# Batch 0's u built transposed in PSUM, with its token form by two DMA transposes, and channel weights loaded in three-chunk pieces

## The chip, the cores and the metric

The kernel runs on one core of a Trainium2 chip. A core has five engines with instruction streams of their own: TensorE (PE, matmuls; its weight loads are PEld), VectorE (DVE), ScalarE (ACT), GpSimd (POOL) and SyncE (SP, which here only issues transfers). Matmul results go to PSUM, eight banks of 128 x 512 floats. The metric is device time in microseconds (us).

## The reference, cut to what matters

```python
# linear attention with decay; q, k, v, alpha: (4, 8, 768, 48)
for t in range(S):
    state = alpha[:, :, t, :, None] * state + einsum('bhd,bhe->bhde', k[:, :, t], v[:, :, t])
    y[:, :, t] = einsum('bhd,bhde->bhe', q[:, :, t], state)
x = y.transpose(0, 2, 1, 3).reshape(B, S, H * D)          # (4, 768, 384)
# mixer
h  = np.maximum(x.transpose(0, 2, 1) @ w_tok1, 0.0) @ w_tok2   # over tokens, 768 -> 256 -> 768
u  = x + h.transpose(0, 2, 1)
h2 = np.maximum(u @ w_ch1, 0.0) @ w_ch2                        # over channels, 384 -> 1536 -> 384
out = u + h2
```

## The kernel before, in words

There are four batches b. Each has three attention chunks of 256 tokens, n = 3b to 3b + 2, whose outputs are six x tiles of 128 tokens by 384 channels (x0_n and x1_n), and then one mixer pass.

`attention(n)` loads alpha, k, q and v (ld_at, ld_kt, ld_qt, ld_vt). The first three chunks take the "wide" form: the log of alpha (ln, ScalarE), a cumulative sum by matmul (cumw), its exponentials E and IE, the scaled keys and queries kk and qq, their TensorE transposes trk and trq with the copies evk and evq, the products G0 and G1 with their masks, the state K with sa and sm, and y0, y1 with the parts from the former state (ia, ib). vb, vs, ka, kb and kc are casts and half turns of v and k. Chunks 6 to 11 transpose by DMA instead (dk, dq).

`mixer(b)` has these operations:

- t1_b_m_kc: six matmuls for each of two halves m of the 256 token features; ht_b_m is the ReLU.
- t2_b_i: for each token tile i, two matmuls into one bank, tokens on the partitions; u_b_i, on VectorE, adds x and writes u.
- The channel product needs u with channels on the partitions (ut). Batch 0 (the tuple UP) does this with TensorE transposes, up_0_p, 18 in all, and three copies ut_0_p. Batches 1 to 3 use two DMA transposes ux_b_half on SP's queue.
- c1_b_mc_half: three matmuls for each of twelve chunks mc of 128 channel features and each half of the tokens; rt_b_mc_half is its ReLU, on ScalarE or VectorE.
- c2_b_i_q4: twelve matmuls for token tile i in four groups; o_b_i adds u (VectorE), st_b_i stores. The last batch's tile 0 is done in two column halves (0h0, 0h1).

Weights come by ldw_ (384 KB each) and are cast by cw_: wt1 in two pieces, wt2 in two (by its 256 input rows), wc1 in six (128 input rows by 768 columns; pieces 0 to 2 are the left half of the columns, 3 to 5 the right), wc2 in six. A c1 of mc below 6 needs wc1 pieces 0, 1 and 2, the others 3, 4 and 5. Loads and weights share 19 raw buffers ("in"); a load waits until its buffer's former use is over.

Nothing is scheduled on the chip. ORDER is a list written out by a planner: each word is an operation and the engine that runs it (t PE, s ACT, v DVE, g POOL, y SP), so each engine's own sequence is that of its words in the list. BUFS gives the buffer numbers. The words f1_, f2_, f3_, f4_, f8_ are filler matmuls on zeros (`fill`, N units of 512 columns), placed ahead of the operation named. Operations marked port=True on VectorE and GpSimd are put one behind the other where the engine changes (`shared`).

Of the kernel before, what the change touches and what calls it, by code (L numbers as in the profile page):

```python
# [9 lines left out]
BF16 = mybir.dt.bfloat16  # L10
# [84 lines left out]
B, H, S, D = 4, 8, 768, 48  # L95
# [6 lines left out]
UP = (0,)  # L102
# [18 lines left out]
def build(g):  # L121
# [194 lines left out]
    def mixer(b):  # L316
# [27 lines left out]
        uts = []
        if b in UP:
            for p in range(3):
                bank = V("one")
# [4 lines left out]
                uts.append(P.op(f"ut_{b}_{p}", either(dve(768, True), act(768)), m0 + (3950 + 340 * p) * sc, writes=[ut],
                                reads=[bank], preds=[o], emit=lambda e, p=p, bank=bank: g.utev(e, ut, bank, p)))
        else:
            for half in range(2):
# [4 lines left out]
        rts = []  # L360
        for mc in range(NDC):
            rt = V("rt")
            ro = []
            for half in range(2):
                bank = V("one")
                o = P.op(f"c1_{b}_{mc}_{half}", pe([384] * 3), m0 + (4900 + 975 * mc + 487 * half) * sc, writes=[bank],
                         reads=[ut], preds=(uts[0:2 + half] if b in UP else [uts[half]]) + [wl[("wc1", p)] for p in ((0, 1, 2) if mc < 6 else (3, 4, 5))],
# [5 lines left out]
        for i in range(NS):  # L373
            hold = 4000.0 if (i >= NS - 3 and b < B - 1) else 0.0
            cuts = [(0, HD // 2), (HD // 2, HD)] if (b, i) == LAST else [(0, HD)]
            for ci, (ca, cz) in enumerate(cuts):
# [3 lines left out]
                for q4 in range(4):  # L380
                    pp = []
                    for mc in range(3 * q4, 3 * q4 + 3):
# [6 lines left out]
                          reads=[bank, us[i][0]], preds=[prev],  # L389
# [25 lines left out]
trq2t ld_at3y vs1_2g ldw_wt11y evq2v ib1t y1_1t y0_1t vs0_2g ldw_wt21y sm1_1g P3g K2t sa0_2v sm0_2g x0_1s t1_0_0_0t
f1_G0_2t G0_2t ldw_wt20y G1_2t cw_wt20g t1_0_1_0t mask0_2v x1_1s t1_0_1_1t ld_at4y ld_kt3y t1_0_1_2t lnP3s cum3t
cw_wt11s IE3s ia2t y0_2t x0_2s t1_0_0_1t t1_0_0_2t E3s t1_0_0_3t mask1_2v t1_0_1_3t ib2t y1_2t ldw_wc14y t1_0_1_4t
x1_2s t1_0_0_4t f1_t1_0_1_5t t1_0_1_5t ht_0_1v P4g cw_wt21s t1_0_0_5t ht_0_0s f3_t2_0_0t t2_0_0t t2_0_1t u_0_0v ln13s
r13s ldw_wc13y t2_0_2t u_0_1v t2_0_3t u_0_2v t2_0_5t lnP4s t2_0_4t u_0_3v u_0_5v u_0_4v up_0_0t cw_wc14s cw_wc13s
ldw_wc15y up_0_1t ld_qt3y k0a3g kk3g cum4t trk3t cw_wc15g ut_0_0v up_0_2t ut_0_2v ut_0_1s c1_0_11_0t c1_0_8_0t IE4s  # L420
c1_0_11_1t rt_0_8_0v rt_0_11_0v ldw_wc11y q0r3g qq3g c1_0_9_1t rt_0_9_1v ln14s kb3s c1_0_10_0t cw_wc11s c1_0_9_0t
# [544 lines left out]
```

## Time and profile before

The median of three runs is 163.35 us (163.22 to 163.51). The profiled execution has a span of 160.5 us from its first to its last instruction, 2.85 us below that median; what lies outside the span is in the time of a run.

| engine | busy us | share of the span | instructions |
|---|---|---|---|
| TensorE matmuls | 154.6 | 96% | 1563 |
| VectorE | 114.9 | 72% | 206 |
| ScalarE | 97.8 | 61% | 179 |
| GpSimd | 80.8 | 50% | 94 |

In the profile, L with a number is a line of the kernel: a group is named by line, engine, operation and out<-in. Through helpers many operations share a line; L643 is every small matmul and the fillers, L902 is c1, L907 c2, L878 t1, L883 t2, L894 up, L712 trk and trq. In the view of stages, each engine has its busy us and in brackets its instructions; then come the granted TensorE clock, the DMA share and GB/s. In the timeline, a row is start, length and instruction, in brackets the idle time ahead of it and what ended that. The chain of work is followed back from the last instruction.

### The profile page before, as it was taken

The numbers are of one execution on the slowest core, as the hardware profiler recorded it, in microseconds if no ns is written. First come the engines' busy times: TensorE is split into PE (matmuls) and PEld (weight loads), VectorE is DVE, ScalarE is ACT, GpSimd is POOL, SyncE is SP. The second block draws the span as 40 slices with busy tenths as digits, with TensorE's granted clock in tenths as the row PEclk, the third lists the DMA queues.
The fourth block names the chain that finished last, engine by engine and source line by source line (L and its number), as shares of the span: only waits on it lengthen the run. The fifth ranks groups of instructions, "written<-read, shape, count | busy, mean of one in ns | idle before, by whom it ended". The sixth has DMA issues, their size and how long they took to land.

```text
span 160.5 us, 3971 instructions
## 1 busy us (share of the span) xinstructions
PE 154.6 (96%) x1563; PEld 97.1 (60%) x1563; DVE 114.9 (72%) x206; ACT 97.8 (61%) x179; POOL 80.8 (50%) x94
## 2 busy tenths in 40 slices
PE   7999989999999999999999999999999999999992
PEld 2545565766667676666667666566567665665661
DVE  6099994979889787989969758795886762464222
ACT  3789999998899955897563583269832203343000
POOL 5205897695973649389778852699523000000000
PEclk9999999999999999999999999999999999999999
DMA  4999999999999999999989999989701235111133
GB/s 122 320 324 317 317 374 311 339 333 306 316 347 324 275 278 272 210 228 319 241 202 298 239 315 204 217 196 134 196 21 62 87 79 169 49 49 53 49 129 116
DMA packets 76130, 35.05 MB, mean 218 GB/s; under 512 B 70352, under 2 KB 74320, under 8 KB 76112
## 3 DMA queue, kind: packets, MB, share of 16 engines
q1 hardware_dynamic: 73808, 31.76, 74.1%
q10 hardware_dynamic: 2304, 3.05, 5.3%
q8 instruction: 12, 0.20, 0.5%
q14 instruction: 6, 0.05, 0.1%
HBM read 25.17 MB, written 4.72 MB: 186 GB/s over the span
## 4 chain that ended last, share of the span: by engine, by line
PE 61%; DMA 12%; DVE 6%; ACT 6%; SPq 6%; POOL 4%; issue 3%; DVEq 0%; POOLq 0%
PE ps L907 22%; PE ps L902 21%; PE ps L643 11%; DMA in<-in_v_dram 6%; SPq L584 6%; DMA out_dram<-o 4%; PE ps L878 3%; PE ps L883 2%; DMA ut<-u 2%; DVE pkk L700 2%; DVE gtm L770 1%; PE ps L712 1%; DVE rt L875 1%; POOL vb L746 1%; POOL pkq L700 1%
## 5 line engine op out<-in xcount | busy, mean ns | idle before, releaser
L907 PE MATMUL ps<-wc,rt 128*128 128x384 bf16 (+1 forms) x300 | 52.4, 319 | 0.0
L902 PE MATMUL ps<-ut,wc 128*128 128x384 bf16 x288 | 50.3, 326 | 0.1
L902 PEld LDWEIGHTS <-wc 128*128 128x128 bf16 x288 | 27.1, 98 | 17.9 <-DMA ut<-u 0.6
L907 PEld LDWEIGHTS <-rt 128*128 128x128 bf16 x300 | 27.8, 98 | 16.0
L873 ACT ACTIVATE rt<-ps 128x384 bf16<-128x384 f32 x47 | 21.4, 492 | 23.6 <-PE ps L902 23.3
L875 DVE TENSOR_SCALAR rt<-ps 128x384 bf16<-128x384 f32 x49 | 25.6, 551 | 9.1 <-PE ps L902 8.9
L770 DVE TENSOR_TENSOR gtm<-ps,mk 128x1024 bf16<-128x1024 f32 x24 | 28.5, 1218 | 3.1 <-PE ps L643 2.8
L911 DVE TENSOR_TENSOR o<-ps,u 128x384 f32<-128x384 f32 (+1 forms) x25 | 13.2, 536 | 12.6 <-PE ps L907 10.1
L700 POOL TENSOR_TENSOR pkk<-in,IE 128x768 bf16<-128x768 f32 x8 | 14.5, 1817 | 3.3 <-DVE ss L844 2.3
L745 ACT CAST x<-ps 128x384 bf16<-128x384 f32 x20 | 9.2, 479 | 11.1 <-PE ps L643 9.5
L887 DVE TENSOR_TENSOR u<-ps,x 128x384 bf16<-128x384 f32 x24 | 12.0, 550 | 3.1 <-PE ps L883 2.5
L746 POOL CAST vb<-in 64x384 bf16<-64x384 f32 (+1 forms) x14 | 8.3, 594 | 10.4 <-DMA in<-in_v_dram 4.7
L692 POOL TENSOR_TENSOR in<-in,in 128x384 f32<-128x384 f32 x8 | 8.0, 1000 | 10.5 <-DVE u L887 3.8
L643 PE MATMUL ps<-rt 128*128 128x512 bf16 (+1 forms) x29 | 12.1, 515 | 1.1 <-DVE rt L541 1.1
L745 ACT CAST vb<-in 64x384 bf16<-64x384 f32 (+1 forms) x18 | 11.4, 634 | 0.8 <-DMA in<-in_v_dram 0.3
L700 POOL TENSOR_TENSOR pkq<-in,E 128x768 bf16<-128x768 f32 x6 | 10.9, 1818 | 0.6 <-DMA tpk<-pkq 0.3
L878 PE MATMUL ps<-x,wt 128*128 128x384 bf16 x48 | 11.0, 325 | 0.0
L844 POOL TENSOR_TENSOR ss<-tmp,E 128x384 bf16<-128x384 f32 x10 | 8.3, 833 | 4.2 <-DVE in L628 3.9
L841 DVE TENSOR_TENSOR tmp<-ps,ss 128x384 f32<-128x384 f32 x16 | 8.8, 552 | 1.8 <-PE ps L643 0.6
L883 PE MATMUL ps<-ht,wt 128*128 128x384 bf16 x48 | 9.1, 326 | 0.0
L643 PE MATMUL ps<-vb,gtm 128*128 128x48 bf16 x192 | 8.2, 183 | 0.2 <-DVE gtm L770 0.2
L643 PE MATMUL ps<-tpq,tpk 48*64 48x128 bf16 (+1 forms) x288 | 7.9, 218 | 0.4 <-POOL tpq L746 0.3
(94 smaller groups left out, 207.6 us busy)
## 6 DMA issues: line engine op xcount, KB each, us to landing
in<-in_alpha_dram SPq DMA_DIRECT2D x12, 384.0 KB, 5.1
in<-in_v_dram SPq DMA_DIRECT2D x12, 384.0 KB, 5.6
in<-in_k_dram SPq DMA_DIRECT2D x12, 384.0 KB, 5.2
in<-in_q_dram SPq DMA_DIRECT2D x12, 384.0 KB, 5.5
in<-in_moe_w_ch_dram SPq DMA_DIRECT2D x12, 384.0 KB, 5.9
out_dram<-o ACTq DMA_DIRECT2D x15, 192.0 KB, 1.8
in<-in_moe_w_tok_dram SPq DMA_DIRECT2D x4, 384.0 KB, 6.0
out_dram<-o SPq DMA_DIRECT2D x8, 192.0 KB, 2.2
```

Of the source, the lines that this page charges most:

```text
L643: return self.pe.matmul(out, lhsT=lhsT, rhs=rhs, start=start, stop=stop, skip_group_check=True)
L700: self.shared(self.eng[e].tensor_tensor(self.t(dst)[:, :, h0:h1, 0:D], self.t(src)[:, h0:h1].rearrange("p h s d -> p s h d"), bass.AP(tens ...
L745: return self.act.copy(d, s)
L770: self.nc.vector.tensor_tensor(self.t(gtm)[:, hf, :, :], self.pair(gp).rearrange("p a (j t) -> p (a j) t", t=128), bass.AP(tensor=m.tensor ...
L873: self.act.activation(d, s, AF.Relu)
L875: self.nc.vector.tensor_scalar_max(d, s, 0.0)
L878: self.pe.matmul(self.bank(bank)[:, 0:HD], lhsT=self.wt1[:, kc, m * 128 : m * 128 + 128], rhs=self.t(x), start=(kc == 0), stop=(kc == NS - 1))
L883: self.pe.matmul(self.bank(bank)[:, 0:HD], lhsT=self.wt2[:, kc, i * 128 : i * 128 + 128], rhs=self.t(hts[kc]), start=(kc == 0), stop=(kc = ...
L887: self.nc.vector.tensor_tensor(self.t(u)[:, i % 3], self.bank(bank)[:, 0:HD], self.t(x), ALU.add)
L902: self.pe.matmul(self.bank(bank)[:, 0:HD], lhsT=self.wc1[:, kc, mc * 128 : mc * 128 + 128], rhs=self.t(ut)[:, 3 * half : 3 * half + 3, kc, ...
L907: self.pe.matmul(self.bank(bank)[:, 0 : cz - ca], lhsT=self.t(rts[mc][0])[:, i * 128 : i * 128 + 128], rhs=self.wc2[:, mc, ca:cz], start=( ...
L911: self.nc.vector.tensor_tensor(self.t(o)[:, ca:cz], self.bank(bank)[:, 0 : cz - ca], self.t(u)[:, i % 3, ca:cz], ALU.add)
```

## The change

For batch 0 alone (UDIR), u is no longer made with tokens on the partitions. For each half of the tokens and each of three channel groups j, one bank takes three matmuls of x against the identity (xa_0_half_j, 128 columns each), which put x in transposed, and then two matmuls of 384 columns of ht against wt2 (tt_0_half_j), which add h transposed. The copy ut_0_half_j (ScalarE or VectorE) writes it as ut. The u that o needs comes from two DMA transposes of ut on SP's queue (un_0_half), put side by side in the queue. t2, u, up and the old ut of batch 0 are gone; the other batches keep theirs.

wc1 is loaded in pieces of 256 columns with all three chunks of 128 input rows, and wt2 in two pieces by output tokens. A c1 needs only the piece of its mc // 2, a t2 or tt only that of its half. The contiguous runs are 1 KB and 1.5 KB instead of 3 KB.

ORDER and BUFS are new from the first word to the last. The fillers are fewer (21 units instead of 36), loads come in another order, many operations change their engine, stores on SP fall from nine to five, and the DMA transposes stand closer together in SP's queue.

```diff
-UP = (0,)
+UP = ()
+UDIR = (0,)
...
+        if b in UDIR:
+            ut, us, uts = V("ut"), [], []
+            for half in range(2):
+                evs = []
+                for j in range(NM):
...
+                    xa = P.op(f"xa_{b}_{half}_{j}", pe([128] * 3), ..., writes=[bank],
+                              reads=[v for v, _ in tx], preds=[o for _, o in tx], ...)
+                    o = P.op(f"tt_{b}_{half}_{j}", pe([384] * 2), ..., writes=[bank],
+                             reads=[h for h, _ in hts], preds=[h for _, h in hts] + [xa, wl[("wt2", half)]], ...)
+                    evs.append(P.op(f"ut_{b}_{half}_{j}", either(act(384), dve(384)), ..., writes=[ut], reads=[bank], preds=[o], ...))
+                uts.append(evs)
                 u = V("u")
+                un = P.op(f"un_{b}_{half}", {"SP": (1240.0, 1240.0)}, ..., writes=[u], reads=[ut], preds=evs, ...)
+                us += [(u, un)] * 3
...
-    ... + [wl[("wc1", p)] for p in ((0, 1, 2) if mc < 6 else (3, 4, 5))],
+    ... + [wl[("wc1", mc // 2)]],
...
-            c, h = piece % 3, piece // 3
-            self.gated(dma(t, self.w[2][128 * c : 128 * c + 128, 768 * h : 768 * h + 768]), op)
+            w = self.w[2].rearrange("(c p) m -> p c m", p=128)
+            self.gated(dma(t.rearrange("p (c m) -> p c m", c=3), w[:, :, 256 * piece : 256 * piece + 256]), op)
...
+    def xadd(self, bank, xs, j):
+        for i, x in enumerate(xs):
+            self.mm(self.bank(bank)[:, i * 128 : i * 128 + 128], self.t(x)[:, j * 128 : j * 128 + 128], self.idn, i == 0, False)
+
+    def tok2t(self, bank, half, j, hts):
+        for kc in range(NDT):
+            self.mm(self.bank(bank)[:, 0:HD], self.t(hts[kc])[:, j * 128 : j * 128 + 128],
+                    self.wt2[:, half, kc, :], False, kc == NDT - 1)
+
+    def utev3(self, e, ut, bank, half, j):
+        self.copy(e, self.t(ut)[:, 3 * half : 3 * half + 3, j, :], self.bank(bank)[:, 0:HD].rearrange("p (i t) -> p i t", i=3))
+
+    def unat(self, u, ut, half):
+        self.nc.sync.dma_start_transpose(self.t(u).rearrange("p i (j c) -> p (i j) c", j=NM),
+                                         self.t(ut)[:, 3 * half : 3 * half + 3].rearrange("p i j t -> p (i j t)"))
```

The order up to the first c1 of batch 0, before:

```
ld_at1y ld_at0y ln1s ln0s f8_cumw1t f1_cumw1t cumw1t IE1s cumw0t IE0s ld_vt0y E0s vb0g vs0_0g vs1_0v ld_kt0y kk0v
f8_trk0t f1_trk0t trk0t E1s ld_qt0y qq0v ka0s kb0s kc0v f1_trq0t trq0t ld_kt1y kk1v K0t evq0s s0_0v ld_vt1y vb1s
f1_trk1t trk1t ld_at2y evk0v ln2s f2_G0_0t G0_0t ld_qt1y ka1g sa1_0v f4_cumw2t cumw2t mask0_0v vs0_1s kb1g kc1g vs1_1s
K1t sm1_0g qq1v sa0_1v sm0_1v G1_0t ld_kt2y IE2s E2s trq1t evq1s ib0t mask1_0v f3_y1_0t y1_0t y0_0t evk1v G0_1t sa1_1v
ld_qt2y x1_0s mask0_1v G1_1t ld_vt2y x0_0s vb2s kk2g trk2t kc2s ldw_wt10y qq2g cw_wt10s f2_ia1t ia1t mask1_1v evk2s
trq2t ld_at3y vs1_2g ldw_wt11y evq2v ib1t y1_1t y0_1t vs0_2g ldw_wt21y sm1_1g P3g K2t sa0_2v sm0_2g x0_1s t1_0_0_0t
f1_G0_2t G0_2t ldw_wt20y G1_2t cw_wt20g t1_0_1_0t mask0_2v x1_1s t1_0_1_1t ld_at4y ld_kt3y t1_0_1_2t lnP3s cum3t
cw_wt11s IE3s ia2t y0_2t x0_2s t1_0_0_1t t1_0_0_2t E3s t1_0_0_3t mask1_2v t1_0_1_3t ib2t y1_2t ldw_wc14y t1_0_1_4t
x1_2s t1_0_0_4t f1_t1_0_1_5t t1_0_1_5t ht_0_1v P4g cw_wt21s t1_0_0_5t ht_0_0s f3_t2_0_0t t2_0_0t t2_0_1t u_0_0v ln13s
r13s ldw_wc13y t2_0_2t u_0_1v t2_0_3t u_0_2v t2_0_5t lnP4s t2_0_4t u_0_3v u_0_5v u_0_4v up_0_0t cw_wc14s cw_wc13s
ldw_wc15y up_0_1t ld_qt3y k0a3g kk3g cum4t trk3t cw_wc15g ut_0_0v up_0_2t ut_0_2v ut_0_1s c1_0_11_0t
```

and after, to where the weights catch up:

```
ld_at0y ln0s f8_cumw0t f1_cumw0t cumw0t ld_at2y ln2s E0s cumw2t ld_qt0y qq0v f2_trq0t trq0t ld_kt0y IE0s kk0v ka0v
kb0v IE2s ld_vt1y vb1g ld_vt0y vb0g vs1_0g vs0_0g vs0_1g evq0s trk0t evk0v G1_0t mask1_0v vs1_1s kc0s G0_0t mask0_0v
ld_at1y ln1s E2s cumw1t IE1s ld_kt2y kk2v K0t s0_0v y0_0t f2_ib0t ib0t y1_0t E1s ld_kt1y kk1v kb1s ld_qt1y qq1v sa1_0v
sm1_0g ka1s f1_trk1t trk1t kc1s trk2t evk2v ld_qt2y qq2g trq1t evq1v x1_0s evk1s K1t sa0_1v sm0_1g f4_G0_1t G0_1t
mask0_1v kc2s ld_vt2y vb2s vs0_2g sa1_1v sm1_1g f2_trq2t trq2t x0_0s ia1t ldw_wt10y ldw_wt20y G1_1t evq2s ld_at3y P3g
y0_1t x0_1s K2t cw_wt10s mask1_1v sa0_2v sm0_2g f1_G0_2t G0_2t ib1t y1_1t x1_1s G1_2t ln13s t1_0_1_0t xa_0_0_0t
t1_0_0_0t t1_0_0_1t t1_0_0_2t t1_0_1_1t t1_0_1_2t ia2t mask0_2v y0_2t lnP3s cum3t ib2t ldw_wt11y cw_wt11s t1_0_0_3t
IE3s mask1_2v vs1_2g y1_2t x1_2s E3s ldw_wt21y xa_0_0_2t x0_2v t1_0_1_3t t1_0_1_4t t1_0_0_4t t1_0_1_5t t1_0_0_5t
ht_0_0s xa_0_1_0t xa_0_1_2t xa_0_0_1t xa_0_1_1t cw_wt21g cw_wt20g ht_0_1v tt_0_1_2t tt_0_0_1t tt_0_0_0t tt_0_0_2t
tt_0_1_1t ld_kt3y ldw_wc10y k0a3v r13s ut_0_0_1s kk3v tt_0_1_0t trk3t ut_0_0_2s cw_wc10g ld_qt3y q0r3g ut_0_0_0v
c1_0_0_0t c1_0_1_0t ldw_wc12y cw_wc12s c1_0_5_0t ut_0_1_2v evk3v ut_0_1_0s ut_0_1_1v c1_0_5_1t rt_0_5_1v ldw_wc15y
```

Later words of the new order: the loads from the 23rd are vt3, at4, wc14, wc13, at5, kt4 and wc11; SP's queue has "ld_at6y un_0_1y un_0_0y ld_at7y" with "o_0_4v", "o_0_3v" and "o_0_2v" among them and mask0_5v behind; ahead of ux_2_0y it has all loads but qt11, and st_0_4 and st_1_1, before two stores just ahead of ux_2, are gone from there.

More of the change, by code (lines that the diff above doesn't have):

```diff
@@ L366, in mixer @@
                 o = P.op(f"c1_{b}_{mc}_{half}", pe([384] * 3), m0 + (4900 + 975 * mc + 487 * half) * sc, writes=[bank],
[L367 removed]
+                         reads=[ut], preds=(uts[half] if b in UDIR else uts[0:2 + half] if b in UP else [uts[half]]) + [wl[("wc1", mc // 2)]],
                          emit=lambda e, mc=mc, half=half, bank=bank: g.ch1(bank, ut, mc, half))
@@ L415 @@
[L415 to L419, printed above, removed]
```

201 lines of the change are left out of this document (106 added, 95 removed), and 22 rows, old and new, of the table BUFS.

## The prediction

> **What bounds the kernel now.** I read the page's busy line first, then busy time by stage, then TensorE's timeline through the first 32 us, and there the other engines and the loads.
>
> ```profile
> span 160.5 us, 3971 instructions
> PE 154.6 (96%) x1563; PEld 97.1 (60%) x1563; DVE 114.9 (72%) x206; ACT 97.8 (61%) x179; POOL 80.8 (50%) x94
> ```
>
> ```profile
> 1.06:31.76 30.70, 29.45 (x318) 16.61 (x319) 23.13 (x51) 26.13 (x40) 18.00 (x25) 1.00 1.06 313
> 31.76:157.44 125.68, 125.19 (x1246) 80.44 (x1246) 91.20 (x153) 71.46 (x140) 62.38 (x64) 1.00 0.75 200
> 157.44:160.50 3.06, 0.00 (x0) 0.00 (x0) 0.36 (x1) 0.00 (x0) 0.00 (x0) 1.00 0.27 96
> ```
>
> From 31.76 us, where the channel product of batch 0 begins, TensorE (first busy column) stands still for 125.68 - 125.19 = 0.49 us until its last matmul. The amount of real matmul work hardly changes, so the time follows from when that packed stretch begins and whether it stays packed. Ahead of it TensorE only looks busy, because of the filler matmuls, which read rt:
>
> ```profile
> 1.06 4.21 PE L643 MATMUL ps<-rt 128*64 128x384 f32 x7 [1.06 <-DVE rt L541]
> ...
> 7.34 2.26 PE L643 MATMUL ps<-rt 128*64 128x384 f32 x7
> 9.73 0.62 PE L712 MATMUL ps<-idn,pkk 128*128 128x128 bf16 x8
> ...
> 25.58 0.37 PE L643 MATMUL ps<-vb,gtm 128*128 128x48 bf16 x8
> ...
> 26.94 0.86 PE L643 MATMUL ps<-rt 128*64 128x384 f32 x2
> 27.73 2.28 PE L883 MATMUL ps<-ht,wt 128*128 128x384 bf16 x12
> 29.85 0.83 PE L894 MATMUL ps<-idn,u 128*128 128x128 bf16 x12
> 30.52 0.33 PE L643 MATMUL ps<-la,u 128*128 128x384 bf16 x1
> ...
> 30.81 0.61 PE L712 MATMUL ps<-idn,pkk 128*128 128x128 bf16 x8
> 31.25 0.50 PE L894 MATMUL ps<-idn,u 128*128 128x128 bf16 x6
> 31.76 0.48 PE L902 MATMUL ps<-ut,wc 128*128 128x384 bf16 x2
> ```
>
> The opening is set by VectorE and by the loads:
>
> ```profile
> 8.33 0.35 DVE L746 CAST vb<-in 64x384 bf16<-64x384 f32 x1 [4.26 <-POOL vb L746]
> 8.72 0.96 DVE L700 TENSOR_TENSOR pkk<-in,IE 128x768 bf16<-128x768 f32 x1
> 12.21 0.68 DVE L746 COPY tpk<-ps 128x1024 bf16<-128x1024 bf16 x1
> 12.80 0.55 DVE L841 TENSOR_TENSOR tmp<-ps,ss 128x384 f32<-128x384 f32 x1
> ...
> 23.17 2.36 DVE L770 TENSOR_TENSOR gtm<-ps,mk 128x1024 bf16<-128x1024 f32 x2
> 26.88 0.56 DVE L875 TENSOR_SCALAR ht<-ps 128x384 bf16<-128x384 f32 x1 [1.36 <-PE ps L878]
> 28.27 2.88 DVE L887 TENSOR_TENSOR u<-ps,x 128x384 bf16<-128x384 f32 x6 [0.83 <-PE ps L883]
> ```
>
> ```profile
> 4.28 0.84 ACT L637 ACTIVATE la<-in 128x768 bf16<-128x768 f32 x1 [2.19 <-DMA in<-in_alpha_dram]
> 6.32 0.81 ACT L687 ACTIVATE IE<-ps 128x768 f32<-128x768 f32 x1
> 11.26 1.31 ACT L745 COPY tpq<-ps 128x1024 bf16<-128x1024 bf16 x1 [0.47 <-PE ps L712]
> 25.99 0.48 ACT L745 CAST x<-ps 128x384 bf16<-128x384 f32 x1
> 30.72 0.80 ACT L745 COPY ut<-ps 128x768 bf16<-128x768 bf16 x1 [0.17 <-PE ps L894]
> ```
>
> ```profile
> 18.61 1.82 POOL L700 TENSOR_TENSOR pkq<-in,E 128x768 bf16<-128x768 f32 x1
> 23.37 0.83 POOL L844 TENSOR_TENSOR ss<-tmp,E 128x384 bf16<-128x384 f32 x1
> 30.16 0.88 POOL L746 CAST wc<-in 128x768 bf16<-128x768 f32 x1 [0.36 <-DMA in<-in_moe_w_ch_dram]
> ```
>
> The first load lands at 4.28. The cast at 30.16 had waited for wc15, the 22nd load in the queue, so a load lands every (30.16 - 4.28) / 21 = 1.23 us, and the nth at about 4.28 + 1.23 (n - 1). VectorE works without a gap from 8.33 (vs1_0) to the end of the third chunk's masks at 25.53. Before, c1_0 with mc of 6 or more needs wc13, wc14 and wc15, thus it could not begin before 30.16 + 0.88 = 31.04, whatever the transposes did.
>
> **The change part by part.** *The opening, walked by hand through the new order, with these durations.* The log of at0 ends at 5.15, cumw0 at 6.3 (5.17 to 6.32 before), E0 (0.83) at 7.15. qt0 is now third (6.74), so qq0 runs 7.2 to 8.15, 1.5 us ahead of the first product before. kk0 9.1, trk0 9.7, evk0 10.4; evq0 on ScalarE (trq0 8.8, then 1.31) 10.1; G1_0 10.9, its mask (2.36 / 2) 12.1, the next 13.3, kk2 14.2. at1 is only seventh (11.66): log 12.5, cumw1 13.65, IE1 14.5. Then VectorE is packed: s0_0 14.7, kk1 15.6, qq1 16.5, sa1_0 17.0, evk2 17.65, evq1 18.9, sa0_1 19.4, mask0_1 20.6, sa1_1 21.1, mask1_1 22.3, sa0_2 22.8, mask0_2 23.9, mask1_2 25.1. On GpSimd sm1_0, qq2 (1.82) and sm0_1 end at 17.8, 19.65 and 20.5, just in time. y1_2 (0.37) 25.45, x1_2 25.95. Before, the last x ended at 26.47: 0.5 us is gained, of a 1.5 us earlier start, because at1 comes late.
>
> *Tail of batch 0's token product.* Before, 27.73 - 26.47 = 1.26 us pass from x1_2 to the first t2; the same gives 27.2 for the first tt. Twelve tt matmuls take what twelve t2 took (29.85 - 27.73 = 2.1): 29.3, trk3 (31.25 - 30.81 = 0.44) 29.7. The eighteen up transposes are gone from here (0.67 + 0.51 = 1.2 us). The eighteen xa matmuls of 128 columns cost 1.0 at the pace of the up transposes (0.67 / 12 each), in the two waits, for the last x and for ht, where the filler of 26.94 stood; without that cover 1.0 comes back. VectorE loses six u additions (2.9) and two ut copies and takes three of the six new ones; ScalarE one ut (0.80) for three like x (0.48 each). None of that ends last.
>
> *Weights in three-chunk pieces.* c1_0_0 and c1_0_1 need only wc10, the 19th load: 26.4, and its GpSimd cast, which stands behind kk3 on VectorE (28.45), ends at 29.3. So c1_0 starts at 29.7 instead of 31.76. cum4, 30.81 - 30.52 = 0.29, is then still to do: the lead is 2.06 - 0.29, some 1.8 us. Runs of 1 KB and 1.5 KB in place of 3 KB I put at nothing:
>
> ```profile
> in<-in_moe_w_ch_dram SPq DMA_DIRECT2D x12, 384.0 KB, 5.9
> in<-in_moe_w_tok_dram SPq DMA_DIRECT2D x4, 384.0 KB, 6.0
> ```
>
> wt1 already comes in 1 KB runs and lands in about the time of the 3 KB ones; the bounds are -0.1 and +0.1 us a load, hidden but for the pieces waited for. The next pieces keep up:
>
> ```profile
> 70.74 2.44 PE ps L902 x15
> ```
>
> A ch1 group of three costs 2.44 / 5 = 0.49. wc15 (22nd, 30.1 plus 0.9 of cast) is wanted after four groups, at 31.65. The tightest is wc11, the 29th: 38.7 plus 0.9, wanted after 18 groups, trq3, the two G of chunk 3 (0.8) and cum4, at 29.7 + 8.8 + 0.4 + 0.8 + 0.3 = 40.0.
>
> *Fillers.* 36 units of 512 columns become 21 (N in fN). Fifteen fewer, at the 2.26 / 9 us of the second row above, are 3.8 us. That is the most the opening can give; the walk turns about half of it into idle time.
>
> *The two un transposes* stand in SP's queue behind ld_at6 and ahead of ld_at7.
>
> ```profile
> 59.29 1.61 SPq L584 DMA_DIRECT2D in<-in_v_dram  x1
> 62.89 1.33 SPq L725 DMA_TRANSPOSE tpk<-pkk  x1
> ...
> 85.63 2.17 SPq L584 DMA_DIRECT2D in<-in_v_dram  x1
> ...
> 93.33 3.16 SPq L624 DMA_DIRECT2D out_dram<-o  x2
> 96.97 3.29 SPq L729 DMA_TRANSPOSE ut<-u  x2
> ```
>
> ```profile
> DMA to landing us min/median/max: 2.8/3.0/3.8
> ```
>
> Two take 3.29 us of issue in the last of the queue's rows, and land 3.0 us after (the answer for ux). They read ut copies made some 20 us earlier, so they wait for nothing; behind them at7, kt6 and at8 shift by 3.3 us, and o_0_4, o_0_3 and o_0_2 wait for them on VectorE, ahead of mask0_5. at6, the 41st load, is issued near 4.28 + 1.23 * 40 - 5.9 = 47.6, the pair by 50.9, landed by 54. c2_0_2_3, the last product ahead of o_0_2, falls near 54 too. I take nothing; without that cover, up to 3 us of VectorE, part of it on the path.
>
> *Everything else in the order* is moved too: 54 of 96 rt evacuations change engine, four stores leave SP for ScalarE, dk and dq stand closer in SP's queue. The data chains stay the same. The idle time after c1's start was 0.49; for the new order I allow 0.3 more, the bounds being 0.5 less and the whole lead.
>
> The end is o and the half store as before (3.06 us), issued by ScalarE: nothing. Sum: 160.5 - 1.8 + 0.3 = 159.0 of span. The runs' median 163.35 is 2.85 above the profiled span, so 161.85.
>
> **The rivals.** *TensorE runs at half rate in the opening (slower).* The same nine filler units took 4.21 us from 1.06 and 2.26 from 7.34, though the granted clock is 1.00 in both rows: after standing idle the array is slower. In my walk it works only some 2 of 5.2 us from 7.4 to 12.6, where the nine-unit filler stood. If it falls back there, cumw1 costs 1.0 more, trk1, trk2 and trq1 0.5 each, and the four units of f4 ahead of G0_1 another 1.0: about 3 us until 19. That is 163.35 - 1.5 + 3 = 164.8. It decides once it lasts past about 17 us. Against it: no single gap in the walk is over 1.5 us. The Trainium skill, "TensorE: Matmul & The Clock Gate", Part 1: The HAM clock gate, has the array fall to half rate after an idle window of about 3.4 us, which would leave it at full rate here and the time at 161.85. Its section "A second HAM failure mode: psum-queue depth-cycling" says that frequent short idles can do it too, which would give this rival's time. This case's trace shows the cold start alone.
>
> *The queue of transfers becomes the bound.* Before ux_2_0 SP has 63 loads (62 before) and two more transposes: 1.23 + 3.29 = 4.5 us more. Two stores ahead of ux_2 (3.16, the row at 93.33) leave the queue. Net 1.4 later, while TensorE wants it 1.5 earlier: 163.35 - 1.5 + 2.9 = 164.75 if SP has no slack; with the slack that it shows (from 60.9, the end of the row at 59.29, it stands 2.0 us ahead of dk6), about 163.3. For it: the loads run at their pace between the rows of 85.63 and 93.33 five loads take 7.7 us of issue. Against: those waits move with the compute.
>
> *The opening starts no earlier*: c1_0 still waits for casts, and only the 0.5 us of x1_2 stays: 162.9.
>
> **How the numbers follow.** Forecast 0.58 (160.4, where most of the 3.8 us shows, to 162.9); half rate 0.17 (164 to 165.5); queue 0.20 (163.0 to 164.75; of it 0.02 faster, 0.06 same, 0.12 slower); no earlier 0.05 (0.03 faster, 0.02 same). With 0.01 of the forecast on the slow side: faster 0.62, same 0.08, slower 0.30. 0.2% is about what a measurement can tell from no change. The range of 8 in 10 is 160.4 to 164.6.
>
> **What would show it.** Right: qq0 near 7.2, the last mask of chunk 2 near 25, the first ch1 matmul near 29.7, its cast just before, less than 1 us of idle from there to the last matmul. Half rate: cumw1's four large products near 13 us taking twice what cumw0's take near 5. Queue: ch1 of batch 2 waiting for ut. The un pair: VectorE's o waiting for a transfer into u near 55 us. The prediction is wrong if the packed stretch starts by 30 but is itself more than 1.5 us longer than 125.7.

## The result, and the profile after

The changed kernel takes 170.57 us (median of 4 runs, 168.88 to 170.97) where the kernel before took 163.28 (162.63 to 163.51) beside it: 1.044 times as long, 95% interval 1.0383 to 1.0498. The prediction was 161.85 with a range of 160.4 to 164.6; the time lies well above it. The profiled execution took 170.76 us, its span is 169.1. Where single executions of a kernel took more than 1.5% longer than its fastest, the times and ratios from here on leave them out.

In the changed kernel lines stand lower down: the matmul helper L643 is now L669, c1 L902 is L944, c2 L907 is L949, o L911 is L953, the copies L745/L746 are L771/L772, the loads L584 are L608, dk and dq L725 are L751, ux L729 is L755, and un is the new L939. First the page's busy line, then busy time by stage (the first pair after the time is the stage's length and TensorE's busy time; the last three numbers are granted clock, DMA share and GB/s).

```profile
span 169.1 us, 3962 instructions
PE 154.6 (91%) x1552; PEld 98.0 (58%) x1552; DVE 111.2 (66%) x197; ACT 97.2 (57%) x180; POOL 83.9 (50%) x99
```

```profile
1.06:30.66 29.60, 26.50 (x301) 16.74 (x302) 22.68 (x49) 23.10 (x36) 14.31 (x24) 0.94 1.07 310
30.66:165.94 135.28, 128.06 (x1255) 81.25 (x1252) 87.99 (x146) 73.80 (x145) 69.14 (x71) 0.99 0.77 192
165.94:169.10 3.16, 0.00 (x0) 0.00 (x0) 0.36 (x1) 0.00 (x0) 0.00 (x0) 1.00 0.42 152
```

TensorE is busy for the same 154.6 us as before. The opening is 1.10 us shorter (30.66 against 31.76), the end 0.10 longer, and the stretch that was packed grew from 125.68 to 135.28: -1.10 + 9.60 + 0.10 = 8.6, which is the difference of the spans. In that stretch TensorE now stands still 135.28 - 128.06 = 7.22 us, against 0.49; the other 2.87 us of the 9.60 are busy time. Its timeline shows where; the bracket names the idle time ahead of a row and what ended it.

```profile
56.25 0.40 PE L669 MATMUL ps<-tpq,tpk 48*128 48x128 bf16 x8 [0.68 <-DVE o L953]
...
69.41 0.34 PE L669 MATMUL ps<-vb,pkk 128*128 128x96 bf16 x4 [1.69 <-ACT pkk L771]
...
73.89 5.52 PE L944 MATMUL ps<-ut,wc 128*128 128x384 bf16 x33 [0.41 <-DMA ut<-u]
...
84.65 0.64 PE L669 MATMUL ps<-tpq,tpk 48*64 48x128 bf16 x32 [0.49 <-POOL tpq L772]
...
92.11 0.90 PE L949 MATMUL ps<-wc,rt 128*128 128x384 bf16 x3 [2.25 <-DVE o L953]
...
122.46 0.64 PE L669 MATMUL ps<-tpq,tpk 48*64 48x128 bf16 x32 [1.09 <-ACT tpq L771]
```

Behind the stand of 2.25 us the granted clock falls to half, and 3.5 us pass at 0.53 of the clock, which is some 1.6 us lost, and more than half of that added busy time:

```profile
90.00:92.50 2.50, 0.39 (x3) 0.19 (x2) 1.00 (x3) 0.41 (x2) 1.26 (x2) 0.97 1.10 271
92.50:96.00 3.50, 3.40 (x51) 2.14 (x50) 2.61 (x4) 2.52 (x4) 1.79 (x3) 0.53 1.03 292
```

Who is late? Five of these six stands lead back to a DMA transpose that landed late. The sixth (92.11) leads to an o tile, whose former content VectorE had to see stored first, with a late transpose right behind it. Here is SP's queue (start, time to issue), and then what VectorE, ScalarE and GpSimd waited for (total, times, longest):

```profile
48.02 6.05 SPq L939 DMA_TRANSPOSE u<-ut  x2
...
60.54 2.08 SPq L608 DMA_DIRECT2D in<-in_v_dram  x1
63.46 2.06 SPq L751 DMA_TRANSPOSE tpk<-pkk  x1
...
74.17 2.68 SPq L608 DMA_DIRECT2D in<-in_alpha_dram  x2
76.94 3.36 SPq L751 DMA_TRANSPOSE tpk<-pkq  x1
...
83.69 2.33 SPq L608 DMA_DIRECT2D in<-in_v_dram  x2
86.37 2.11 SPq L751 DMA_TRANSPOSE tpk<-pkk  x1
```

```profile
DVE o L953 <- DMA out_dram<-o: 4.3, 2, 2.6
...
ACT pkk L771 <- DMA tpk<-pkk: 2.4, 1, 2.4
ACT tpq L771 <- DMA tpk<-pkq: 2.3, 1, 2.3
...
POOL tpq L772 <- DMA tpk<-pkq: 1.6, 1, 1.6
...
DVE o L953 <- DMA u<-ut: 1.0, 1, 1.0
```

The answers for single issues give 7.1 and 4.2 us from issue to landing for the un pair, 5.4 for dk6 (63.46), 6.3 for dq7 (76.94), 6.7 for dk8 (86.37) and 6.2 for the dk at 113.46. The two lines below group all dk and dq, the first of the kernel before, the second of the changed one:

```profile
DMA to landing us min/median/max: 2.7/3.0/5.9
```

```profile
DMA to landing us min/median/max: 2.8/3.6/6.7
```

Before, the latest landing (5.9) was that of the dq at 104.16, right behind the load at 103.65:

```profile
103.65 0.42 SPq L584 DMA_DIRECT2D in<-in_q_dram  x1
104.16 1.87 SPq L725 DMA_TRANSPOSE tpk<-pkq  x1
```

In the changed kernel the six that take longer than 5.2 us are all issued within 0.9 us of the end of a load's issue. The dq at 115.94 (5.1) stands behind the late dk of 113.46; the stand at 122.46 comes by way of it.

### The profile page after: what moved, and what is told of

It is laid out like the page before. It is cut to its first block, busy times and chain, and to the rows that moved or that the text cites. A ratio compares the mean times of both kernels' runs of the same rounds, so it can differ in the third digit from the quotient of the medians.

```text
span 169.1 us, 3962 instructions
## 1 busy us (share of the span) xinstructions
PE 154.6 (91%) x1552; PEld 98.0 (58%) x1552; DVE 111.2 (66%) x197; ACT 97.2 (57%) x180; POOL 83.9 (50%) x99
## 4 chain that ended last, share of the span: by engine, by line
PE 58%; DMA 23%; DVE 3%; ACT 2%; POOL 2%; SPq 2%; issue 1%; DVEq 0%
PE ps L949 19%; PE ps L944 16%; PE ps L669 13%; DMA tpk<-pkk 7%; DMA tpk<-pkq 7%; PE ps L904 5%; DMA u<-ut 4%; PE ps L909 3%; DMA in<-in_q_dram 2%; DMA ut<-u 2%; PE ps L738 2%; SPq L751 2%; ACT tpq L771 2%; POOL pkk L726 1%; DVE o L953 1%
## 5 line engine op out<-in xcount | busy, mean ns | idle before, releaser
L949 PE MATMUL ps<-wc,rt 128*128 128x384 bf16 (+1 forms) x300 | 54.8, 323 | 2.3 <-DVE o L953 2.3
L944 PE MATMUL ps<-ut,wc 128*128 128x384 bf16 x288 | 51.7, 326 | 0.6 <-DMA ut<-u 0.6
L899 ACT ACTIVATE rt<-ps 128x384 bf16<-128x384 f32 x51 | 23.8, 491 | 28.9 <-PE ps L944 27.8
L949 PEld LDWEIGHTS <-rt 128*128 128x128 bf16 x300 | 28.0, 98 | 18.8 <-issue 3.0
L944 PEld LDWEIGHTS <-wc 128*128 128x128 bf16 x288 | 26.9, 98 | 18.3 <-issue 0.9
L901 DVE TENSOR_SCALAR rt<-ps 128x384 bf16<-128x384 f32 x45 | 23.6, 553 | 17.0 <-PE ps L944 16.9
L953 DVE TENSOR_TENSOR o<-ps,u 128x384 f32<-128x384 f32 (+1 forms) x25 | 13.0, 538 | 16.2 <-PE ps L949 10.9
L870 POOL TENSOR_TENSOR ss<-tmp,E 128x384 bf16<-128x384 f32 x13 | 10.9, 836 | 17.9 <-DVE tmp L867 11.3
L726 POOL TENSOR_TENSOR pkq<-in,E 128x768 bf16<-128x768 f32 x8 | 14.5, 1814 | 0.6
L771 ACT CAST vb<-in 64x384 bf16<-64x384 f32 (+1 forms) x20 | 13.0, 656 | 2.7 <-DVE o L953 2.1
L772 POOL CAST vb<-in 64x384 bf16<-64x384 f32 (+1 forms) x16 | 8.9, 563 | 8.1 <-DVE kt L772 7.4
L669 PE MATMUL ps<-tpq,tpk 48*64 48x128 bf16 (+1 forms) x288 | 8.8, 228 | 3.4 <-ACT tpq L771 1.3
L771 ACT CAST x<-ps 128x384 bf16<-128x384 f32 x16 | 7.5, 474 | 6.6 <-PE ps L669 6.5
L726 POOL TENSOR_TENSOR pkk<-in,IE 128x768 bf16<-128x768 f32 x6 | 10.9, 1817 | 0.7 <-ACT IE L705 0.5
L669 PEld LDWEIGHTS <-tpk 48*64 48x64 bf16 (+1 forms) x288 | 6.5, 108 | 7.3 <-issue 4.0
L913 DVE TENSOR_TENSOR u<-ps,x 128x384 bf16<-128x384 f32 x18 | 8.8, 549 | 1.2 <-PE ps L909 1.2
L669 PE MATMUL ps<-rt 128*128 128x512 bf16 (+1 forms) x18 | 8.6, 582 | 1.1 <-DVE rt L565 1.1
L669 PE MATMUL ps<-vb,gtm 128*128 128x48 bf16 x192 | 9.0, 188 | 0.0
L654 POOL TENSOR_TENSOR in<-in 128x384 f32<-128x384 f32 x8 | 7.9, 998 | 1.0 <-DVE in L718 0.8
```

The source lines that it names most:

```text
L669: return self.pe.matmul(out, lhsT=lhsT, rhs=rhs, start=start, stop=stop, skip_group_check=True)
L726: self.shared(self.eng[e].tensor_tensor(self.t(dst)[:, :, h0:h1, 0:D], self.t(src)[:, h0:h1].rearrange("p h s d -> p s h d"), bass.AP(tens ...
L771: return self.act.copy(d, s)
L772: return self.shared(self.eng[e].tensor_copy(d, s))
L870: self.shared(self.eng[e].tensor_tensor(self.st(self.t(s)), self.st(self.t(t)), self.amul(E, hf, wide), ALU.mult))
L899: self.act.activation(d, s, AF.Relu)
```

## The experiments

The theory that this suggests, "behind loads": a DMA transpose that SP issues right after loads lands in 5 to 7 us and not in 3, and the new order puts the un pair, dk6, ux_1, dq7, dk8 and one dk at 113 in that place. The rivals: transposes side by side slow each other; the un pair alone moved everything; o and its stores; the half clock.

**The cost by itself.** A kernel that only issues groups of transposes and loads, fully drained in between.

```diff
+CASES = ("T", "TT", "TTT", "LT", "LLT", "LLLLT", "LLLLTT", "TLLLL", "LLLLTLLLL", "LLTLLT", "WWWWT", "T")
```

> Nothing of the reference is computed here: only DMA transposes (T, 128 x 1024 of bf16, as dk and dq) and loads (L, 384 KB of q, k, v or alpha; W, of the channel weights) are issued from SP's queue, in groups with a full drain between them: T; TT; TTT; LT; LLT; LLLLT; LLLLTT; TLLLL; LLLLTLLLL; LLTLLT; WWWWT; T. Theory 'behind loads': a transpose by itself lands some 2.8 us after its issue (the median of before), in TT and TTT all land in 3 to 3.6, and what stands behind loads lands the later the more of them are outstanding: LLT 4 to 5, LLLLT and LLLLTT 5 to 7; in TLLLL the T keeps its 2.8. Rival 'side by side': T behind loads keeps 2.8 to 3.3 in all groups, and it is the second and third T of TT and TTT that land in 5 to 7 us.

Landing, in us: T 3.1; TT 3.2, 3.1; TTT 3.3, 3.5, 3.2; LT 4.1; LLT 4.9; LLLLT 4.7; LLLLTT 4.8, 3.2; TLLLL 3.2; LLLLTLLLL 4.7; LLTLLT 4.6, 4.7; WWWWT 6.1; T 3.0. (The median of dk and dq before is 3.0, as shown above, not the 2.8 of the expectation.) SP's rows of LT, LLT and LLLLT (line numbers of that kernel) show that the issue grows too, from the 1.24 to 1.34 of a transpose with nothing ahead:

```profile
19.92 1.70 SPq L41 DMA_TRANSPOSE tp<-pk  x1
...
26.16 2.61 SPq L41 DMA_TRANSPOSE tp<-pk  x1
...
35.49 2.40 SPq L41 DMA_TRANSPOSE tp<-pk  x1
```

Side by side costs nothing; behind loads costs 1.0 to 1.8 us, and 3.0 behind weights, less than "behind loads" had said for four loads, since its price does not grow past two of them. What follows the transpose does not matter (TLLLL).

**The same in the kernel before**, one move (the diffs of the order show SP's words alone, without the engine's letter):

```diff
 ld_qt8 ld_at10
+ld_vt8 ld_at11 ld_qt9
 dk8 dq7 dk7 st_0_2 dq8
-ld_vt8 ld_at11 ld_qt9
```

> The kernel before with one thing of the new order: the loads vt8, at11 and qt9 stand ahead of dk8, dq7 and dk7 in SP's queue, not behind them (their buffers are long free). Theory 'behind loads': dk8 lands in 5 to 7 us after its issue instead of 2.7 to 3.0, and TensorE, which stood 0.49 us in the whole packed stretch, stands 1 to 4 us more near 80 to 86: 164 to 167. Rival 'side by side': nothing changes at dk8; 163.0 to 163.7.

169.41 us (167.56 to 169.87) against 162.02 to 164.32 (163.18) of the kernel before beside it, ratio 1.0372 (1.0295 to 1.0449): more than either theory gave. dk8 lands in 5.2 us. SP, GpSimd and TensorE:

```profile
79.64 2.94 SPq L725 DMA_TRANSPOSE tpk<-pkk  x1
```

```profile
87.00 0.50 POOL L746 COPY pkk<-pkk 64x384 bf16<-64x384 bf16 x1 [6.31 <-DMA tpk<-pkk]
```

```profile
87.55 0.34 PE L643 MATMUL ps<-vb,pkk 128*128 128x96 bf16 x4 [3.56 <-POOL pkk L746]
```

dk8, dq7 and dk7 are late one behind the other, and the copy of kc7 waits for the last of them. The medians lie 6.2 us apart, where the whole change costs 7.3. Not all of it is shown to be the move's. The profile is of the fastest execution (167.56). In it TensorE is already 1.25 us behind the kernel before at its first c1 (33.01), which the move does not touch. Matmul for matmul it is 1.46 us behind at 79.4, and 5.2 to 5.6 us from behind the stand at 87.55 on. So some 3.9 us are the move's there. The 1.25 stay unexplained; executions of the kernel before differ by more. Part of the price is the issue of the three loads itself: dk8 is issued 4.05 us later than before (75.59), 1.46 of which was there already.

**The changed kernel without the un pair.**

```diff
-emit=lambda e, u=u, half=half: g.unat(u, ut, half)
+emit=lambda e: None
```

> The changed kernel without the two transposes that make batch 0's token form: o of batch 0 adds u in its transposed form instead, which costs the same and gives other values in batch 0's output. All else is in the changed order. Theory 'behind loads' (the transposes land late because of the loads issued just ahead of them, and un is only two of them): the 6.05 us of SP's queue at 48 us are gone, with them TensorE's 0.68 at 56 us and, since loads at7 to vt7 now come 6 us earlier and have landed by the time dk6 is issued, the 1.69 and 0.41 at 69 to 74; dq7, dk8 and dk10 still stand right behind loads, so the 0.49 at 84.65, the 2.25 with the half clock behind it at 92, and the 1.09 at 122 stay: 170.6 - 2.8 = 167.8, and 167 to 169. Rival 'it is the un pair': everything downstream follows from the shift of the loads by 6 us, and the packed stretch comes back to some 126.5 us: 162 to 163.5.

This kernel leaves out the making of the token form; o adds ut as it lies, so batch 0's output is not that of the reference. 169.16 us, ratio 1.0385 (1.031 to 1.046), 0.2 us above the theory's range. The stands at 56, 69 and 74 are gone as expected, but 0.96 us for dq7 remain (6.6 us to land), and the one at 90 grew to 3.77, with 0.54 of the clock from 89 to 96.5: the time saved ahead was given back there. The rival that un alone moves everything falls.

**The loads behind the transposes, in part** (at9, at10; vt8, kt10, vt9; qt11):

```diff
-ld_at9 ld_at10 dq7 dk7 dq8 ld_kt10 ld_vt9 ld_vt8 dk8
+dq7 dk7 dq8 ld_at9 ld_at10 dk8 ld_vt8 ld_kt10 ld_vt9
```

> The changed kernel with loads taken from in front of transposes in SP's queue: at9 and at10 behind dq7, dk7 and dq8; vt8, kt10 and vt9 behind dk8; qt11 ahead of ux_2_0 (vb9, ln1 and r1 of chunk 10 move behind their loads). The un pair and dk6 stay as they are. Theory 'behind loads': dq7, dk8 and dk10, which landed in 6.3, 6.7 and 6.2 us, land in 2.8 to 3.6; TensorE's 0.49 at 84.65 and 1.09 at 122.5 go, and of the 2.25 at 92 with its half clock what follows from kc7 standing late: 170.6 - 1.6 to - 5.3, so 165.3 to 169. Rival 'side by side': they land as late as before, being as near to each other as before, and the time is 170 to 171.5. Rival 'o and its stores': the landing gets short, but the 2.25 at 92 and the half clock stay, since o waits for a store: 168.5 to 169.5.

168.44 us, ratio 1.0372 (1.026 to 1.0484), near the upper end of the theory's range. dq7, dk7, dq8 and dk8 land in 4.6, 4.0, 2.7 and 3.9 us (dq7 still behind qt8 and kt8), and the stands at 84.65 and 122.46 are gone. But ScalarE now waits for vt8 and vt9, and TensorE stands 3.34 us at 94.83: a new wait in place of the old one, for loads that now come too late.

**Three single edits, and their sum.** Eight filler units more in the opening; the stores st_0_1 and st_0_5 earlier and the o tiles in turn; the loads behind 60 us set out anew among the transposes. The third edit is less than its expectation says: three loads still stand right ahead of dq7 and three right ahead of dk8.

```diff
+f1_trk0 ... f3_G1_0 ... f4_cumw1
```

> The changed kernel with eight more units of filler matmuls in the opening: one ahead of trk0, three ahead of G1_0, four ahead of cumw1, where TensorE stood idle some 2.5 us between 8 and 13 us. Theory 'half rate in the opening': the clock stays at 1.00 from 13 to 17 us, the first channel matmul comes 0.8 to 1.2 us earlier than the 30.66 of the changed kernel, and the packed stretch keeps its stalls: 170.6 - 1.0 = 169.6, and 169.0 to 170.0. Rival 'the opening has slack' (the loads and VectorE set it): the clock is 1.00 but the first channel matmul stays within 0.3 us of 30.4, 170.0 to 171.

```diff
 st_0_0
+st_0_1 st_0_5
...
-st_0_5 ... st_0_1
```

> The changed kernel with the stores st_0_1 and st_0_5 moved up in ScalarE's queue to stand behind st_0_0, and the three o tiles given out in turn, so that o_1_0, o_1_1 and o_1_3 no longer go through one tile while two others wait for their late stores. Transposes and loads stay as they are. Theory 'behind loads': VectorE's wait of 2.59 us at 91.5 goes, but dk8, issued behind three loads, still lands near 93, so that TensorE stands about as long a little later: 169.3 to 170.8. Rival 'o and its stores': TensorE's 2.25 us at 92 and the half clock behind it (1.7 us) both go: 166.5 to 167.5.

```diff
-ld_kt7 ld_vt7 dk6 ux_1_0 ld_qt7 ux_1_1 dq6 ld_qt8 ld_kt8 ld_at9 ld_at10 dq7 dk7 dq8 ld_kt10 ld_vt9 ld_vt8 dk8
+ld_kt7 dk6 ux_1_0 ld_qt7 ux_1_1 dq6 ld_vt7 ld_qt8 ld_kt8 dq7 dk7 dq8 ld_vt8 ld_at9 ld_at10 dk8 ld_kt10 ld_vt9
```

> The changed kernel with nearly all loads taken from in front of the transposes behind 60 us: vt7 behind dq6, qt7 behind ux_1_0, vt8, at9 and at10 behind dq8, kt10 and vt9 behind dk8, qt11 ahead of ux_2_0; what reads these loads (casts, logarithms, products) moves behind them, and vb9 on ScalarE behind vs0_8, which in the run with fewer moves it had held up. The un pair stays. Theory 'behind loads': dq7, dk7 and dk8 land in 2.7 to 4 us, TensorE's stalls of 0.49, 2.25 and 1.09 go or shrink to under 1 us together, the half clock at 92 with them, and dk6 comes back by about 1 of its 1.69: 164.5 to 167. Rival 'another wait takes its place' (the loads, now later, are missed themselves, as vt8 was): 167.5 to 170.

> The three edits together (fillers in the opening, o tiles in turn with earlier stores, loads behind the transposes). If the causes add up: the lead of the opening shows (about 1.8), what is left is the un pair's 0.7 and about 1 us of dk6 and ux_1: 162.0 to 164.0. If one of them hides another, 164 to 167.

Fillers: 170.34, ratio 1.0504 (1.042 to 1.0587). The clock stays at 1.00 in the opening and c1 begins at 29.89, but the time shows no gain: c1 is where the theory put it, the time where the rival did. In the profile the lead of 0.77 us over the changed kernel is gone at dk6, which is waited for longer than without the edit (2.25 against 1.69), with the half clock behind it; 0.5 us of it is back at the last matmul:

```profile
29.89 1.30 PE L944 MATMUL ps<-ut,wc 128*128 128x384 bf16 x7
```

```profile
68.54 0.47 PE L669 MATMUL ps<-vb,pkk 128*128 128x96 bf16 x4 [2.25 <-ACT pkk L771]
```

o tiles: 169.76, ratio 1.0451 (1.0364 to 1.0539). VectorE's wait for the store is gone, and TensorE stands at the same place for dk8 itself, 6.5 us after its issue at 86.0. So the wait for the o tile had only covered the wait for dk8:

```profile
92.50 0.73 PE L669 MATMUL ps<-tpq,tpk 48*64 48x128 bf16 x32 [2.45 <-DMA tpk<-pkk]
```

Queue order: 166.32 and 167.43, ratio 1.0262 (1.0169 to 1.0356), in the theory's range or just above it. Its profile is of an execution of 169.41, with the half clock in its opening (c1 at 31.04). There dq7, dk7 and dk8 still land in 6.3, 5.4 and 5.2 us, not in the 2.7 to 4 that were expected, and the stands are 0.33, 1.07, 0.62, 2.03 (an o tile again), 1.18, 0.58, 0.55 and 0.53: shorter, but more of them. So the time came nearly as said, but not by the transposes landing early. All three: 168.19, ratio 1.0368 (1.029 to 1.0446), 4 us or more above what adding up would have given, above the second range too, and no faster than the queue order alone. dq7, dk7 and dk8 land in 6.2, 6.8 and 6.1 behind the loads that the edit leaves there, and 2.13 us at 88.5 with the half clock behind it came of it.

**The parts of the change alone.** Channel weights in three-chunk pieces, in the kernel before:

```diff
-self.gated(dma(t, self.w[2][128 * c : 128 * c + 128, 768 * h : 768 * h + 768]), op)
+self.gated(dma(t.rearrange("p (c m) -> p c m", c=3), w[:, :, 256 * piece : 256 * piece + 256]), op)
```

> The kernel before with one part of the change alone: the channel weights wc1 come in three-chunk pieces (1 KB runs) and each c1 needs only its own piece; order, loads and transposes as before. The prediction put the shorter runs at nothing, with -0.1 to +0.1 us a load as bounds. If that holds: 163.0 to 163.6 (the first c1 stays near 31.8, since it waits for the up transposes as well). Rival 'short runs': the six loads take longer, what is loaded behind them comes 0.6 us or more later, and trk3 and the pieces themselves are waited for: 163.7 to 165.

163.01 against 162.68, ratio 1.0009 (0.9973 to 1.0044): nothing, as predicted. (wt2's two pieces have no run of their own.) Two transposes in the place of the un pair, in the kernel before:

```diff
 ld_at6
+for half in range(2):
+    g.nc.sync.dma_start_transpose(g.T["u"][2 + half].rearrange("p i (j c) -> p (i j) c", j=NM),
+                                  g.T["ut"][0][:, 3 * half : 3 * half + 3].rearrange("p i j t -> p (i j t)"))
```

> The kernel before with two DMA transposes added in SP's queue behind ld_at6, as the un pair stands in the changed kernel (they copy ut of batch 0 into the two u tiles that batch 1 will write; nothing reads the result, and nothing on VectorE waits for them but u_1). Theory 'behind loads': the pair takes 5 to 6 us of SP's queue, the loads behind it come 3 to 5 us later, and dk6 then stands right behind the last of them and lands in 4 to 5.5 us; before's slack ahead of dk6 (2.0 us) is used up: 1 to 3 us of TensorE's idle time at 65 to 72, 164 to 166.5. Rival 'a pair costs its 3.3 us of issue and is hidden', as the prediction had it: 163.0 to 163.7.

165.53, ratio 1.0168 (1.0096 to 1.0239). The pair takes 5.44 us of SP's queue and lands 6.4 and 3.9 us after its issues. The time is that of the theory, the place is not: dk6 lands in 2.7, but the loads of at7 and vt5 come late, GpSimd waits for them, and TensorE stands 2.08 us at 60.22 (with the half clock behind it) and 1.40 at 121.12.

**Without un, u added by matmul.** Three 128-column matmuls of ut with the identity per token tile finish the bank of c2; first in the changed order, then with the fillers, the stores and SP's queue set out anew, and last with what still stalled mended.

```diff
+for j in range(NM):
+    self.mm(self.bank(bank)[:, j * 128 : j * 128 + 128], self.t(ut)[:, i, j, :], self.idn, False, j == NM - 1)
```

> The changed kernel with batch 0's token form not made at all: u is added into the channel product's bank by three 128-column matmuls of ut with the identity per token tile (18 in all), and o is a copy. No un pair, 1.0 us more on TensorE (0.67 per 12 of the up transposes), all else in the changed order. Theory 'behind loads': as in the run without un, the loads come 6 us earlier and dk6 and ux_1 land in time, while dq7 and dk8 still stand behind loads and the stand at 90 stays: 169.2 + 1.0 = 170.2, and 169 to 171. Rival 'VectorE's wait for u moved everything': below 168.

169.75, ratio 1.0406 (1.0352 to 1.0459): as said; dq7 is waited for by 1.19, and 3.75 are lost at 92.

```diff
+... ld_vt7 ld_qt7 ld_qt8 ld_kt8 dk6 ux_1_0 ux_1_1 dq6 ld_vt8 ld_at9 ld_at10 dq7 dk7 dq8 dk8 ld_kt10 ld_vt9 ...
```

> u by matmul, the eight filler units, the o tiles in turn with earlier stores, and the loads of SP's queue put where no transpose is due: qt7, qt8 and kt8 ahead of dk6 (there is room for them without the un pair); dk6, ux_1 and dq6 with no load between; vt8, at9, at10 behind dq6; dq7, dk7, dq8 and dk8 with no load between; kt10 and vt9 behind dk8; vb9 behind vs0_8; qt11 ahead of ux_2_0. Theory 'behind loads': transposes land in 2.7 to 4 us but for dq7 (4 to 6), the packed stretch has under 2 us of stalls and the clock stays at 1.00: 160.5 span from an opening 1.8 us shorter, 1.0 more of matmuls, 1 to 2 of stalls: 162.5 to 164.5. If the time stays above 166, loads ahead of transposes are not what costs the changed kernel its time.

167.24, ratio 1.0245 (1.0193 to 1.0296); 2.7 us over the theory's upper end. By the sign laid down beforehand (above 166) this speaks against the theory. Against that sign stands that the edit did not clear every transpose: in the profile (165.46, the fastest execution) 1.68 us are left for dk6, right behind kt8 and 5.7 us to land. The others are 0.37, 0.80 and 1.20 (dk11, behind dq11). The next run mends these places.

```diff
+... ld_vt7 ld_qt7 dk6 ux_1_0 ux_1_1 dq6 ld_qt8 ld_kt8 ld_vt8 dq7 dk7 dq8 ld_at9 dk8 ld_at10 ld_kt10 ld_vt9 ... dq10 dk11 dq11 ...
```

> As u_by_matmul_reordered, with the places that still stalled mended: qt8 and kt8 go behind dq6, so that only qt7 stands between vt7 and dk6 and SP has done with it 2 to 3 us before dk6 is ready; at9 goes behind dq8 and at10 behind dk8 (P10 and the logarithms of at9 and at10 follow them); dk11 goes ahead of dq11, for which it had waited. Theory 'behind loads': dk6 lands in 2.7 to 4 us instead of 5.7, the stalls of 1.68 at 68.7 and 1.20 at 122 go, span 163.8 - 2.5 = 161.3, times of 162.5 to 164.8 against 167.2. Rival 'something else of the new order': the stalls only move and it stays at 166.5 or more.

> The same, with the un pair put back in its place behind at6 in SP's queue (and the 18 matmuls of ut with the identity gone, 1.0 us of TensorE). If the pair were hidden, this is 1.0 us faster than reordered_2. Theory 'behind loads': the pair takes some 6 us of SP's queue, the loads up to qt7 then end about 64, dk6 stands right behind them again, and the run is 1 to 3 us slower than reordered_2.

165.15 without the pair, 0.35 us over the range expected and well below the rival's 166.5, ratio 1.0189 (1.0147 to 1.0231), and 168.24 with it, ratio 1.036 (1.0308 to 1.0411). dk6 without the pair, and with it:

```profile
62.27 1.38 SPq L748 DMA_TRANSPOSE tpk<-pkk  x1
```

```profile
63.84 3.73 SPq L751 DMA_TRANSPOSE tpk<-pkk  x1
```

```profile
70.49 0.34 PE L669 MATMUL ps<-vb,pkk 128*128 128x96 bf16 x4 [2.95 <-ACT pkk L771]
```

It lands in 3.9 us without and in 6.1 with the pair, which has pushed the loads up against it. The pair costs 3.1 us here although it saves 1.0 us of matmuls. So clearing the transposes and leaving out the pair takes back some 4.3 of the 7.3 us, together with the fillers and the o tiles. No version beat the kernel before. reordered_2 is still 3.0 us slower although its c1 begins at 29.26. What stands in it is 2.75 us of idle time (1.44 and 0.70 of it at 93, waiting for GpSimd) and the 18 matmuls. GpSimd had waited there for a cast of v, and ScalarE's cast for its load, one of those moved behind dk8:

```profile
90.65 0.83 ACT L768 CAST vb<-in 128x768 bf16<-128x768 f32 x1 [2.47 <-DMA in<-in_v_dram]
```

The queue that lets the transposes through makes a load late instead.

**All transposes of all these kernels together** (286 issues behind 44 us in the two kernels and the thirteen variants of them), by the time between the end of SP's last load issue and the issue of the transpose:

| time since the last load issue | issues | landing, min / median / max, us | over 4 us |
|---|---|---|---|
| under 0.5 us | 43 | 4.6 / 6.1 / 7.1 | 43 |
| 0.5 to 2 | 13 | 3.4 / 4.5 / 6.1 | 9 |
| 2 to 3 | 26 | 2.7 / 4.2 / 6.8 | 15 |
| 3 to 4 | 36 | 2.9 / 3.4 / 4.7 | 7 |
| over 4 | 168 | 2.7 / 2.9 / 5.5 | 12 |

The kernel before has one issue in the first row, the changed kernel five, and dk6 (5.4 us) in the second.

## Why the prediction was wrong, point by point

- *The walk through the opening*: right in its mechanism, at most 0.2 us off where the clock stayed up. c1 was to begin at 29.7; without the extra fillers it began at 30.66 in the changed kernel (half rate from 13 to 17 us), at 29.47 and 29.70 in two variants whose clock stayed at 1.00, and at 29.89 with the fillers. *The rival of half rate* was real but worth far less than 3 us: from the start of cumw1 (13.05) to c1 it took 17.61 us in the changed kernel, against 16.98 and 17.12 in those two variants. That is some 0.5 to 0.6 us of half rate; the rest of the difference is a later start of cumw1 (12.49 and 12.58 there).
- *Pieces of weights at nothing*: right for wc1 (1.0009), not tested for wt2. The row it rested on groups wt1 with wt2, which came in 3 KB runs, so it could not show what it was read for.
- *"Two take 3.29 us of issue … and land 3.0 us after"; "I take nothing"*: wrong. Issue was 6.05, landing 7.1 and 4.2, since at6 and the wc2 pieces are right ahead. The sign given for it came: VectorE's o at 55.17 waited 1.03 us for the transfer into u. The pair's price is 0.9 to 1.4 us in the changed order (by the ratios and by the medians; the two intervals overlap, and another stand takes part of it back), 3.1 plus 1.0 in a mended order, and some 2.8 in the kernel before. The row with 3.29 came from a place with two stores ahead and no load within 3.7 us.
- *"The data chains stay the same … I allow 0.3 more idle"*: this is the step that failed the most: 7.22 us of idle time against 0.49 + 0.3, and 1.6 us of half clock. The prediction took a transpose's landing for a constant of the operation (2.8/3.0/3.8). It is set for the most part by what SP has issued just ahead of it, so an order that leaves every data chain alone still makes transposes 2 to 4 us later. The transpose that took 5.9 us to land in the kernel before, its only one right behind a load, stood in the trace; the prediction does not use it.
- *The rival of the queue of transfers* was nearest: SP's queue is what decides, and a lead of the opening can be lost to it (fillers: 0.77 us earlier at c1, nothing gained in the time). Its mechanism was off. It counted loads and pairs up to ux_2 and priced them at 1.4 us there; the loss came at dk6, dq7 and dk8, more from order than from number (without the pair it is still 169.16).
- *The end*: 3.16 against 3.06, as said.
- *From span to time*: the 2.85 us are not all outside the span. In every execution listed here a time is 1.7 to 1.8 us above its span, so some 1.1 of the 2.85 are a profiled execution that was faster than the median. The forecast, being a difference, does not suffer by it.
- What was to show it wrong came all but in full: the stretch began at 30.66, not by 30, but was 9.6 us longer than 125.7, against the 1.5 allowed.

The Trainium skill, "DMA: Bandwidth & Descriptors", section Queues, rings and completion order, says that what SP issues goes to one ring of its own on each DMA engine, and that each ring's descriptors are taken in order. By that a transpose would wait for what is left of the loads ahead of it. The table agrees: 43 of 43 right behind a load landed over 4 us, 12 of 168 with more than 4 us in between.

Not settled: why before_loads_ahead lost 1.25 us in its opening; what makes 7.1 us in the full kernels of the 6.1 at most that the transposes showed by themselves; how much of the 3.0 us left in reordered_2 is SP's queue and how much the rest of the new order, which no run takes apart; and a few transposes that landed late with no load near (next section).

## What to carry to other kernels

In these runs a transposing transfer's time from issue to landing belonged to its place in the queue more than to the operation: before a transpose is moved, look up what its queue issues in the 3 us ahead of it, and ask the trace for its largest landing, not only the median. Two more transfers in a full queue are paid for by what stands behind them, even if nothing waits for the two. A lead won ahead of such a queue may be spent at it. And moving loads out of a transpose's way is only safe for loads that have time to spare: here they became the next wait.

## What the runs showed of the hardware that was not expected

- A DMA transpose alone lands in 3.0 to 3.1 us, the second and third of a group in 3.1 to 3.5; behind two or more loads in 4.6 to 4.9, behind four weight loads in 6.1; in the full kernels up to 7.1. SP's issue of it grows from 1.24 to between 1.7 and 4.6 us, so that the queue behind it stands as well.
- The clock fell to half after stands of TensorE that were shorter than thought: of 2.08, 2.09, 2.13, 2.25 (twice), 2.45, 2.95, 3.34, 3.75 and 3.77 us, but not after 2.03, 2.06 and 3.56. In the opening it fell in 4 of 6 kernels of the changed order, with no single gap over 1.5 us, and in none of 5 with eight more filler units (one profile of each). The Trainium skill, "TensorE: Matmul & The Clock Gate", Part 1: The HAM clock gate, gives an idle window of some 3.4 us that runs freely; the stands of 2.08 to 2.95 are shorter than that, and the one of 3.56 shows that the length alone does not decide.
- One transpose in u_by_matmul_reordered (dk8, issued at 82.94, 9 us after SP's last load issue) landed 5.5 us later though the stage row of its first microsecond (DMA share and GB/s last) shows the DMA engines at rest. No run explains it.

```profile
83.00:84.00 1.00, 1.00 (x41) 0.71 (x30) 0.90 (x2) 0.80 (x2) 0.94 (x2) 1.00 0.00 0
```
